# Gathering an expert's rows by quarters of channels and turning them on VectorE in squares of 32, in a fused attention and mixture-of-experts kernel

## The chip, the cores and the metric

The kernel runs on one core of a Trainium2 chip. The metric is the device time of one execution in microseconds (us), the median of several runs, each beside a run of the other kernel. The profiles shown are of one execution each; their times are measured from the first instruction to the last and are a little shorter than the device time.

The engines are named as in the profile: PE (TensorE, matrix products and transposes), PEld (its weight loads), DVE (VectorE), ACT (ScalarE), POOL (GpSimd) and SP (SyncE, which here only issues transfers). A fp32 product of one 128x128 block stands as two matmul instructions in the profile, so the counts there are twice those of the code; transposes stand once.

## The reference

Attention with a window of 96 tokens and 8 global tokens comes first (batch 4, 8 heads, 768 tokens, 64 channels per head), then a router that sends each of the 3072 tokens to one of 8 experts, then that expert's two matrix products. All data are fp32.

```python
def _attn_ref(q, k, v, n_global, n_local):
    ...
    scores = scale * np.matmul(q, k.transpose(0, 1, 3, 2))     # + bias by distance, masked
    a = np.exp(scores - max)                   # softmax over the kept keys
    return np.matmul(a / sum, v)

# x: attention's output as (3072 tokens, 512 channels)
def _moe_ref(x, expert_emb, tau, w1, w2):                      # w1: 8 x 512 x 1024, w2: 8 x 1024 x 512
    ...
    logits = xn @ en.T / tau                                   # rows of x and expert_emb normalized
    expert_idx = np.argmax(logits, axis=1)
    gate_w = probs[np.arange(N), expert_idx]                   # probs: softmax of logits
    for e in range(E):
        mask = expert_idx == e
        h = np.maximum(x[mask] @ w1[e], 0.0)
        out[mask] = gate_w[mask, None] * (h @ w2[e])
    return out
```

## The kernel before

Attention works through 32 steps (4 batches, 2 groups of heads, 4 parts). Beside them, each finished batch is turned to rows of tokens, divided by its softmax sums, stored to DRAM (`x_dram`), and routed. The router (`choose`) gives each token a slot in a table in DRAM (`meta`): expert times `SL` plus the token's rank in the expert. An entry has three numbers: row in x_dram, row in the output, gate. GpSimd scatters the entries.

```python
    slot = new([n], "slot", I32)
    nc.vector.scalar_tensor_tensor(out=slot, in0=best, scalar=16.0 * k.SL, in1=rank, op0=ALU.mult, op1=ALU.add)
    gate = new([n], "gate")
    nc.vector.reduce_sum(out=gate, in_=lg, axis=AX.X)
    nc.vector.tensor_scalar_add(gate, gate, 1e-9)
    mt = new([n, 3], "mt")
    nc.vector.reciprocal(out=mt[:, :, 2], in_=gate)
    nc.gpsimd.tensor_copy(out=mt[:, :, 0:2], in_=k.tok[:, b * k.NT + i0 : b * k.NT + i0 + n, :])
    for t in range(n):
        i = nc.gpsimd.indirect_dma_start(
            out=k.meta[:], out_offset=bass.IndirectOffsetOnAxis(ap=slot[:, t : t + 1], axis=0),
            in_=mt[:, t, :], in_offset=None,
        )
...
    def store_x(t, i, ps):
        xs = xs_p.tile([P, H, D], F32, name="xs", tag="xs")
        nc.vector.tensor_tensor(out=xs[:], in0=ps[:].rearrange("p (h d) -> p h d", d=D),
                                in1=t.rd[:, i, :].unsqueeze(2).broadcast_to([P, H, D]), op=ALU.mult)
        flat = xs[:].rearrange("p h d -> p (h d)")
        r0 = t.b * S + t.b // (B - 1) + i * P
        nc.sync.dma_start(k.x_dram[r0 : r0 + P, :], flat)
        nc.scalar.activation(k.junk[:], flat, AF.Square, accum_out=t.ss[:, i : i + 1])
```

The last batch is routed in two halves. Expert 0 takes its first 256 tokens (`FIRST`) as soon as the first three batches are routed; their first product fills TensorE while the last half is routed. `k.base` holds how many slots expert 0 has served that way.

```python
    def first_base():
        k.base = k.const.tile([P, E], F32, name="base")
        nc.vector.memset(k.base[:], 0.0)
        nc.vector.tensor_scalar(out=k.base[:, 0:1], in0=k.cnt[:, 0:1], scalar1=float(FIRST), scalar2=None, op0=ALU.min)
        k.si = k.const.tile([P, 1], I32, name="si")
        nc.vector.tensor_copy(out=k.si[:], in_=k.base[:, 0:1])

    def first_rows():
        k.first = Net()
        k.first.rows = load_rows(k, k.meta[0:FIRST, :], k.ea, k.ea2, FIRST // P, nc.gpsimd, k.ZR + 1)
        k.first.xT = k.ea.tile([P, k.NC, FIRST], F32, name="fxT")
        k.first.hT = k.ea.tile([P, k.NF, FIRST], F32, name="fhT")

    def first_turn():
        for j, xg in enumerate(k.first.rows[2]):
            ps = bank()
            for c in range(k.NC):
                nc.tensor.transpose(ps[:, c * P : (c + 1) * P], xg[:, c * P : (c + 1) * P], k.ident[:])
            nc.scalar.copy(out=k.first.xT[:, :, j * P : (j + 1) * P], in_=ps[:].rearrange("p (c n) -> p c n", c=k.NC))
...
    attend(*steps[-1])                       # the end of attention
    for hf in active:
        half_turns(hf)
    first_turn()
    hf = start_half(t, 1)                    # the last half batch
    xs = [turn_x(t, 3)]
    turn_sums(hf)
    score_experts(hf, bank())
    xs += [turn_x(t, 4), turn_x(t, 5)]
    for i in range(3):
        store_x(t, 3 + i, xs[i])
    ...
    turn_products(hf)
    first_product(0)
    next(hf.router)
    hf.router.send(bank())                   # L210 is in here
    first_product(1)
    next(hf.router)
    ...                                      # first_product(2) to (7)
```

Then the experts run one after the other. For each, the slots' entries are read, up to 512 rows (`CAP`) of x_dram are gathered by token in four tiles of 128 rows, and TensorE turns them to channels on the partitions (`xT`). A switch on the expert's count (`width`, a multiple of 32, or 128) takes a branch with just so many columns.

```python
def load_rows(k, slots, gp, xgp, NJ=CAP // P, cast=None, upto=None):

    nc = k.nc
    mt = gp.tile([P, NJ, 3], F32, name="emt", tag="emt")
    i = nc.sync.dma_start(mt[:], slots.rearrange("(j p) w -> p j w", p=P))
    for sc in k.scatters or []:
        ...                                  # waits for every scatter
    ids = gp.tile([P, NJ, 2], I32, name="ids", tag="ids")
    (cast or nc.vector).tensor_copy(out=ids[:], in_=mt[:, :, 0:2])
    xgs = []
    for j in range(NJ):
        xg = xgp.tile([P, k.DM], F32, name="xg", tag="xg")
        nc.gpsimd.indirect_dma_start(
            out=xg[:], out_offset=None, in_=k.x_dram[0 : upto or k.N + 1, :],
            in_offset=bass.IndirectOffsetOnAxis(ap=ids[:, j, 0:1], axis=0),
        )
        xgs.append(xg)
    return mt, ids, xgs


def turn_rows(k, rows, xT):

    for j, xg in enumerate(rows[2]):
        ps = k.work.tile([P, k.NC, P], F32, name="work", tag="work")
        for c in range(k.NC):
            k.nc.tensor.transpose(ps[:, c, :], xg[:, c * P : (c + 1) * P], k.ident[:])
        k.nc.vector.tensor_copy(out=xT[:, :, j * P : (j + 1) * P], in_=ps[:])
...
def expert(k, rows, xT, w1, w2, width=None, coming=None, behind=None):
    ...
    arms = [len(WIDTHS) - 1] if width is None else tc.Switch(width.index, len(WIDTHS), hint=width.hint)
    for arm in arms:
        w = WIDTHS[arm]
        parts = []
        for size in (64, 32):
            if w % (2 * size) >= size:
                parts.append(part_rows(k, rows, w // (2 * size) * 2 * size, size))
        for f2 in range(k.NF // 2):
            ps = k.big.tile([P, 2, CAP], F32, name="big", tag="big")
            for i in range(2):
                f = 2 * f2 + i
                for c in range(k.NC):
                    nc.tensor.matmul(ps[:, i, 0:w], lhsT=w1[:, c, f * P : (f + 1) * P], rhs=xT[:, c, 0:w],
                                     start=c == 0, stop=c == k.NC - 1)
            nc.scalar.activation(hT[:, 2 * f2 : 2 * f2 + 2, 0:w], ps[:, :, 0:w], AF.Relu)
        if coming:
            turn_rows(k, coming.rows, coming.xT)
        for part in parts:
            second_part(k, part, hT, w2)
        for j in range(0 if behind else 1, w // P):
            second(k, rows, hT, w2, j, k.work)
    if coming:
        coming.width = take_width(k, coming.e)
    if behind:
        behind()
    else:
        second(k, rows, hT, w2, 0, k.work0)
...
        def prepare(e):
            t = Net()
            t.e = e
            at = e * n.SL
            if e == 0:
                at = nc.values_load(n.si[0:1, 0:1], engines=(SP,), min_val=0, max_val=FIRST)
            t.rows = load_rows(n, n.meta[bass.ds(at, CAP), :], n.gp, n.xgp)
            ...                              # from expert 2 on: load its weights
            return t

        with tc.manual_schedule(engines=ORDERED | set(ARMS)):
            choose_widths(n)
            coming = prepare(0)
            coming.width = take_width(n, 0)
            second(n, n.first.rows, n.first.hT, n.w[0][1], 0, n.work)
            coming.xT = n.xtp.tile([P, n.NC, CAP], F32, name="xT", tag="xT")
            turn_rows(n, coming.rows, coming.xT)
            for e in range(n.E):
                now, coming = coming, prepare(e + 1) if e + 1 < n.E else None
                behind = None
                if e == 0:
                    def behind():
                        second(n, n.first.rows, n.first.hT, n.w[0][1], 1, n.work0)
                expert(n, now.rows, now.xT, *now.w, now.width, coming, behind)
```

`manual_schedule` keeps the program's order on each engine. `second` computes 128 rows of the second product on TensorE (L904), scales them by the gate on VectorE (L907) and scatters them to the output by GpSimd (L908); `second_part` does so for the last 64 or 32 rows (L939). If the inputs do not meet what the fast path assumes, a general path (`leftover`) recomputes; with the inputs here it is not entered.

## Time and profile before

| | |
|---|---|
| device time | 589.17 us (588.56 to 589.4, 3 runs) |
| profiled execution | 580.19 us, span 578.5 us |
| TensorE clock granted | 0.971 of full speed on average |
| attention and routing | 0 to 225 us |
| experts 0 to 7 | 225 to 562 us |
| DMA moved | 78.11 MB, 135 GB/s over the span |

Line 1 of the page gives each engine's busy time; line 2 cuts the span in 40 slices and gives the busy share in tenths. In a line of a group, "x128" is the number of instructions, then come busy time in us and mean ns of one, then the engine's idle time before them and what ended it ("<-"). In the chain of work that ended last, each line is a start, a length, and what the time was spent on; one line can merge many instructions.

### The profile page before, as it was taken

Reading aid. Unit: us, or ns where it says so; the run is one execution under the profiler, and the core shown is the slowest. Engines: PE = TensorE matmul, PEld = TensorE weight load, DVE = VectorE, ACT = ScalarE, POOL = GpSimd, SP = SyncE. Lnnn points to the kernel's source line nnn. Section 1 sums busy time; section 2 is a strip of 40 time slices with the busy share of each in tenths; the row PEclk is TensorE's granted clock in tenths of the full one; section 3 lists DMA queues with packets and bytes.
Section 4 is the critical chain, followed back from the end, with each engine's and each line's share of the span. In section 5 each row is a group of like instructions: output and inputs, shape, how many; then the busy total and the mean of one; then the engine's idle time right before and its main releaser. Section 6 shows DMA issues by size and latency. Waiting matters only on the chain.

```text
span 578.5 us, 9188 instructions
## 1 busy us (share of the span) xinstructions
PE 548.2 (95%) x3542; PEld 350.8 (61%) x3542; DVE 164.5 (28%) x411; ACT 142.3 (25%) x336; POOL 101.8 (18%) x130
## 2 busy tenths in 40 slices
PE   8899999999989798999999999999999999999980
PEld 8577788787767676757444447556556444645530
DVE  3254666675775412111000110212101110210010
ACT  4575756756643210001001001001001001001100
POOL 2000015013232225140130013030130130110010
PEclk9799999999989898999999999999999999999995
DMA  8999998994246414543460326443461460010000
GB/s 174 194 186 201 258 254 182 256 235 72 74 128 185 126 25 129 189 150 115 177 238 0 123 84 238 158 142 120 160 232 39 159 226 30 16 43 20 2 36 25
DMA packets 117331, 78.11 MB, mean 135 GB/s; under 512 B 92965, under 2 KB 101157, under 8 KB 117169
## 3 DMA queue, kind: packets, MB, share of 16 engines
q1 hardware_dynamic: 109744, 60.72, 40.9%
q0 software_dynamic: 5536, 15.25, 7.4%
q8 instruction: 51, 0.84, 0.6%
q14 instruction: 112, 0.91, 0.5%
q10 hardware_dynamic: 1888, 0.40, 0.4%
HBM read 63.38 MB, written 13.16 MB: 132 GB/s over the span
## 4 chain that ended last, share of the span: by engine, by line
PE 58%; issue 2%; DMA 1%; POOL 1%; DVE 0%; POOLq 0%
PE big L968 27%; PE work L904 25%; PE work L939 3%; PE work L894 2%; DMA xg<-x_dram,ids 1%; POOL xg L881 0%; POOL out_dram L908 0%; POOL meta L245 0%; DVE y L907 0%; POOLq L1004 0%; DVE flags L1018 0%; POOLq L908 0%; POOLq L881 0%
## 5 line engine op out<-in xcount | busy, mean ns | idle before, releaser
L968 PE MATMUL big<-xT,w1t 128*128 128x320 f32 (+5 forms) x512 | 159.0, 472 | 0.0
L904 PE MATMUL work<-w2t,hT 128*128 128x512 f32 x320 | 139.4, 595 | 0.0
L968 PEld LDWEIGHTS big<-xT,w1t 128*128 128x128 f32 x512 | 95.0, 193 | 64.4 <-issue 31.6
L904 PEld LDWEIGHTS work<-w2t,hT 128*128 128x128 f32 x320 | 60.3, 190 | 74.6 <-issue 73.8
L970 ACT ACTIVATE hT<-big 128x640 f32<-128x640 f32 (+5 forms) x32 | 24.9, 777 | 303.7 <-PE big L968 303.7
L429 DVE TENSOR_TENSOR ex<-ex,table 126x768 f32<-126x768 f32 x64 | 57.7, 904 | 57.9 <-ACT ex L422 55.9
L907 DVE TENSOR_SCALAR y<-work,emt 128x512 f32<-128x512 f32 x22 | 16.5, 751 | 156.7 <-PE work L904 150.0
L422 ACT ACTIVATE ex<-pa 126x384 f32<-126x384 f32 (+1 forms) x128 | 53.3, 476 | 28.8 <-PE pa L418 28.8
L908 POOL DMA_INDIRECT out_dram<-y,ids x22 | 21.8, 992 | 185.6 <-DVE y L907 133.1
L895 DVE COPY xT<-work 128x512 f32<-128x512 f32 x32 | 20.1, 683 | 109.9 <-PE work L894 109.9
L418 PE MATMUL pa<-qT,kT 64*126 64x192 f32 (+1 forms) x512 | 50.7, 336 | 0.4 <-ACT ex L422 0.4
L444 PE MATMUL od<-ex,v 126*64 126x192 f32 (+1 forms) x576 | 48.6, 316 | 0.0
L418 PEld LDWEIGHTS pa<-qT,kT 64*126 64x126 f32 x512 | 41.5, 190 | 10.7 <-issue 6.0
L444 PEld LDWEIGHTS od<-ex,v 126*64 126x64 f32 x576 | 36.0, 142 | 8.8 <-issue 4.7
L881 POOL DMA_INDIRECT xg<-x_dram,ids x34 | 33.3, 981 | 23.0 <-issue 15.6
L245 POOL DMA_INDIRECT meta<-mt,slot x24 | 26.3, 1095 | 38.3 <-DVE good L542 7.8
L452 PE MATMUL od<-ex,halves 126*32 126x192 f32 (+1 forms) x576 | 26.9, 310 | 0.0
L943 POOL DMA_INDIRECT out_dram<-y,pids x7 | 7.1, 1015 | 89.3 <-DVE y L942 84.0
L217 POOL TENSOR_TENSOR ss<-ss,half 128x3 f32<-128x3 f32 (+1 forms) x6 | 6.3, 1047 | 93.0 <-ACT junk L526 93.0
L526 ACT ACTIVATE junk<-xs 128x512 f32<-128x512 f32 x24 | 15.2, 632 | 27.1 <-DVE xs L521 22.2
L939 PE MATMUL work<-w2t,hT 128*32 128x128 f32 (+1 forms) x320 | 20.4, 317 | 0.0
L452 PEld LDWEIGHTS od<-ex,halves 126*32 126x32 f32 x576 | 14.9, 111 | 8.8 <-issue 3.6
(143 smaller groups left out, 389.9 us busy)
## 6 DMA issues: line engine op xcount, KB each, us to landing
w1t<-in_moe_w_dram SPq DMA_DIRECT2D x6, 2048.0 KB, 9.5
w2t<-in_moe_w_dram SPq DMA_DIRECT2D x6, 2048.0 KB, 11.5
v<-in_v_dram SPq DMA_DIRECT2D x32, 192.0 KB, 4.7
x_dram<-xs SPq DMA_DIRECT2D x24, 256.0 KB, 2.8
k<-in_k_dram SPq DMA_DIRECT2D x28, 192.0 KB, 4.0
q<-in_q_dram SPq DMA_DIRECT2D x28, 192.0 KB, 4.2
w1t<-in_moe_w_dram SPq DMA_DIRECT2D x32, 128.0 KB, 3.7
w2t<-in_moe_w_dram SPq DMA_DIRECT2D x32, 128.0 KB, 3.7
```

Source lines behind the costliest of these rows:

```text
L245: i = nc.gpsimd.indirect_dma_start(out=k.meta[:], out_offset=bass.IndirectOffsetOnAxis(ap=slot[:, t : t + 1], axis=0), in_=mt[:, t, :], in ...
L418: nc.tensor.matmul(u.sp[e][0:ROWS, a * n : (a + 1) * n], lhsT=t.kT[rows, j, 0:ROWS], rhs=t.qT[rows, j * BLK : j * BLK + n], start=True, st ...
L422: nc.scalar.activation(u.ex[:, e], u.sp[e][0:ROWS, 0 : 2 * u.n].rearrange("p (a c) -> p a c", a=2), AF.Exp, scale=k.scale)
L429: nc.vector.tensor_tensor(out=exv, in0=exv, in1=tab[:, :, 0 : u.n // BLK, :], op=ALU.mult)
L444: nc.tensor.matmul(g.od[a][e * D : (e + 1) * D, at : at + c1 - c0], lhsT=g.v[0:ROWS, 2 * a + e, u.j, :], rhs=u.ex[:, e, a, c0:c1], start=f ...
L452: nc.tensor.matmul(g.od[2][32 * i : 32 * i + 32, at : at + c1 - c0], lhsT=k.halves[0:ROWS, g.m].rearrange("p i c -> p (i c)"), rhs=u.ex[:, ...
L881: nc.gpsimd.indirect_dma_start(out=xg[:], out_offset=None, in_=k.x_dram[0 : upto or k.N + 1, :], in_offset=bass.IndirectOffsetOnAxis(ap=id ...
L904: nc.tensor.matmul(ps[:], lhsT=hT[:, f, j * P : (j + 1) * P], rhs=w2[:, f, :], start=f == 0, stop=f == k.NF - 1)
L908: nc.gpsimd.indirect_dma_start(out=k.out[:, :], out_offset=bass.IndirectOffsetOnAxis(ap=ids[:, j, 1:2], axis=0), in_=y[:], in_offset=None, ...
L939: nc.tensor.matmul(ps[i * size : (i + 1) * size, 0:m], lhsT=hT[:, f, base : base + size], rhs=w2[:, f, i * m : (i + 1) * m], start=f == 0, ...
L968: nc.tensor.matmul(ps[:, i, 0:w], lhsT=w1[:, c, f * P : (f + 1) * P], rhs=xT[:, c, 0:w], start=c == 0, stop=c == k.NC - 1)
L970: nc.scalar.activation(hT[:, 2 * f2 : 2 * f2 + 2, 0:w], ps[:, :, 0:w], AF.Relu)
```

## The change

An expert's rows are no longer turned by TensorE but by VectorE, which transposes squares of 32 x 32 within groups of 32 partitions. For that to give xT, each group of 32 partitions must hold its own quarter of the channels for 32 tokens. So (1) the rows are gathered in sixteen transfers, each of which brings 32 tokens in four quarter rows of 128 channels (512 bytes), on 4 x 32 partitions; (2) x_dram holds the channels in an order in which a quarter row carries the right 32 of each block of 128, which `store_x` writes in two instructions; (3) the slots of each 256 are stored in an order in which eight entries for one partition lie side by side (`place`), so that the table is read in runs of 96 bytes, four times over, and the entries in slot order (`mt`) are copied from it by four small VectorE instructions; (4) expert 0's own rows and the 256 first ones are still gathered whole and turned by TensorE, after a copy on ScalarE that puts their channels in order (`in_order`); (5) expert 0's second read of the table starts at a static slot (256), for which its count is raised to at least 256 and the table has 256 more slots per expert; (6) the turning of the next expert's rows is issued just ahead of the last tile of `tiles` instead of straight after the first product.

The aim is to take the transposes of experts 1 to 7 off TensorE. The diff, with the general path and pool set-up cut:

```diff
@@ -22,6 +22,7 @@
 PIECES = 32
+UNIT = 256
 FIRST = 256
@@ -75,6 +76,11 @@
     nc.gpsimd.tensor_scalar_add(k.tok[:, last:, 0], k.tok[:, last:, 0], 1.0)
+    k.quad = pool.tile([P, 1], F32, name="quad")
+    nc.gpsimd.memset(k.quad[:], 0.0)
+    for q in range(1, 4):
+        nc.gpsimd.memset(k.quad[32 * q : 32 * q + 32], float(q))
     k.cnt = pool.tile([P, k.E], F32, name="cnt")
@@ -234,6 +240,7 @@
     nc.vector.scalar_tensor_tensor(out=slot, in0=best, scalar=16.0 * k.SL, in1=rank, op0=ALU.mult, op1=ALU.add)
+    slot = place(k, slot, new)
@@ -255,6 +262,17 @@
+def place(k, slot, new):
+    nc = k.nc
+    low, mid = new([slot.shape[1]], "low", I32), new([slot.shape[1]], "mid", I32)
+    nc.vector.tensor_scalar(out=low, in0=slot, scalar1=31, scalar2=3, op0=ALU.bitwise_and, op1=ALU.logical_shift_left)
+    nc.vector.tensor_scalar(out=mid, in0=slot, scalar1=5, scalar2=UNIT // 32 - 1, op0=ALU.logical_shift_right, op1=ALU.bitwise_and)
+    nc.vector.scalar_tensor_tensor(out=mid, in0=slot, scalar=-UNIT, in1=mid, op0=ALU.bitwise_and, op1=ALU.bitwise_or)
+    nc.vector.tensor_tensor(out=low, in0=low, in1=mid, op=ALU.bitwise_or)
+    return low
...
@@ -517,10 +537,12 @@
     def store_x(t, i, ps):
-        xs = xs_p.tile([P, H, D], F32, name="xs", tag="xs")
-        nc.vector.tensor_tensor(out=xs[:], in0=ps[:].rearrange("p (h d) -> p h d", d=D),
-                                in1=t.rd[:, i, :].unsqueeze(2).broadcast_to([P, H, D]), op=ALU.mult)
-        flat = xs[:].rearrange("p h d -> p (h d)")
+        xs = xs_p.tile([P, k.DM], F32, name="xs", tag="xs")
+        flat = xs[:]
+        for e in range(2):
+            dst = flat.rearrange("p (e l c j) -> p e c l j", e=2, l=2, c=4)[:, e]
+            nc.vector.tensor_tensor(out=dst, in0=ps[:].rearrange("p (c e l j) -> p e c l j", c=4, e=2, l=2)[:, e],
+                                    in1=t.rd[:, i, e::2].unsqueeze(2).unsqueeze(3).broadcast_to([P, 4, 2, 32]), op=ALU.mult)
         r0 = t.b * S + t.b // (B - 1) + i * P
@@ -562,11 +584,11 @@
     def first_base():
         k.base = k.const.tile([P, E], F32, name="base")
         nc.vector.memset(k.base[:], 0.0)
-        nc.vector.tensor_scalar(out=k.base[:, 0:1], in0=k.cnt[:, 0:1], scalar1=float(FIRST), scalar2=None, op0=ALU.min)
-        k.si = k.const.tile([P, 1], I32, name="si")
-        nc.vector.tensor_copy(out=k.si[:], in_=k.base[:, 0:1])
+        nc.vector.memset(k.base[:, 0:1], float(FIRST))
+        nc.vector.tensor_tensor(out=k.cnt[:], in0=k.cnt[:], in1=k.base[:], op=ALU.max)
@@ -577,8 +599,10 @@
             ps = bank()
+            xo = k.ea.tile([P, k.DM], F32, name="xo", tag="xo")
+            in_order(k, nc.scalar, xo[:], xg[:])
             for c in range(k.NC):
-                nc.tensor.transpose(ps[:, c * P : (c + 1) * P], xg[:, c * P : (c + 1) * P], k.ident[:])
+                nc.tensor.transpose(ps[:, c * P : (c + 1) * P], xo[:, c * P : (c + 1) * P], k.ident[:])
             nc.scalar.copy(out=k.first.xT[:, :, j * P : (j + 1) * P], in_=ps[:].rearrange("p (c n) -> p c n", c=k.NC))
...
@@ -864,34 +891,71 @@
-def load_rows(k, slots, gp, xgp, NJ=CAP // P, cast=None, upto=None):
-    nc = k.nc
+def load_rows(k, slots, gp, xgp, NJ=CAP // P, cast=None, upto=None, squares=False):
+    nc, U = k.nc, UNIT // 32
+    cast = cast or nc.vector
+    mq = gp.tile([P, NJ * P // UNIT, U, 3], F32, name="mq", tag="mq")
+    for u in range(NJ * P // UNIT):
+        src = slots[u * UNIT : (u + 1) * UNIT, :].rearrange("(i g) w -> i (g w)", g=U)
+        i = nc.sync.dma_start(mq[:, u].rearrange("p g w -> p (g w)"), src.unsqueeze(0).to_broadcast([4, 32, U * 3]))
+        for sc in k.scatters or []:
...
     mt = gp.tile([P, NJ, 3], F32, name="emt", tag="emt")
-    i = nc.sync.dma_start(mt[:], slots.rearrange("(j p) w -> p j w", p=P))
-    for sc in k.scatters or []:
...
+    mqv = mq[:].rearrange("p u (h a) w -> p (u h) a w", a=4)
+    for a in range(4):
+        rows = slice(32 * a, 32 * a + 32)
+        cast.tensor_copy(out=mt[rows], in_=mqv[rows, :, a, :])
     ids = gp.tile([P, NJ, 2], I32, name="ids", tag="ids")
-    (cast or nc.vector).tensor_copy(out=ids[:], in_=mt[:, :, 0:2])
+    cast.tensor_copy(out=ids[:], in_=mt[:, :, 0:2])
+    src = k.x_dram[0 : upto or k.N + 1, :]
+    if squares:
+        qid = gp.tile([P, NJ * 4], I32, name="qid", tag="qid")
+        cast.tensor_scalar(out=qid[:], in0=mq[:].rearrange("p u g w -> p (u g) w")[:, :, 0], scalar1=4.0,
+                           scalar2=k.quad[:], op0=ALU.mult, op1=ALU.add)
+        xq = xgp.tile([P, NJ * 4, P], F32, name="xq", tag="xq")
+        for g in range(NJ * 4):
+            nc.gpsimd.indirect_dma_start(
+                out=xq[:, g], out_offset=None, in_=src.rearrange("t (q m) -> (t q) m", q=4),
+                in_offset=bass.IndirectOffsetOnAxis(ap=qid[:, g : g + 1], axis=0),
+            )
+        return mt, ids, xq
     xgs = []
...
         nc.gpsimd.indirect_dma_start(
-            out=xg[:], out_offset=None, in_=k.x_dram[0 : upto or k.N + 1, :],
+            out=xg[:], out_offset=None, in_=src,
             in_offset=bass.IndirectOffsetOnAxis(ap=ids[:, j, 0:1], axis=0),
...
+def in_order(k, eng, dst, xg):
+    src = xg.rearrange("p (q c j) -> p c q j", q=4, j=32)
+    dst = dst.rearrange("p (c q j) -> p c q j", q=4, j=32)
+    (eng.copy if eng is k.nc.scalar else eng.tensor_copy)(out=dst, in_=src)
 def turn_rows(k, rows, xT):
+    if not isinstance(rows[2], list):
+        n = CAP // 32 // 4
+        for i in range(4):
+            g = slice(i * n, (i + 1) * n)
+            dst = xT[:].rearrange("p c (g i) -> p g c i", i=32)[:, g]
+            k.nc.vector.transpose(dst, rows[2][:, g].rearrange("p g (c j) -> p g c j", j=32))
+        return
     for j, xg in enumerate(rows[2]):
+        xo = k.yp.tile([P, k.DM], F32, name="xo", tag="xo")
+        in_order(k, k.nc.scalar, xo[:], xg[:])
         ps = k.work.tile([P, k.NC, P], F32, name="work", tag="work")
         for c in range(k.NC):
-            k.nc.tensor.transpose(ps[:, c, :], xg[:, c * P : (c + 1) * P], k.ident[:])
+            k.nc.tensor.transpose(ps[:, c, :], xo[:, c * P : (c + 1) * P], k.ident[:])
         k.nc.vector.tensor_copy(out=xT[:, :, j * P : (j + 1) * P], in_=ps[:])
@@ -968,11 +1032,16 @@
             nc.scalar.activation(hT[:, 2 * f2 : 2 * f2 + 2, 0:w], ps[:, :, 0:w], AF.Relu)
-        if coming:
+        tiles = range(0 if behind else 1, w // P)
+        for i, part in enumerate(parts):
+            if coming and not tiles and i == 0:
+                turn_rows(k, coming.rows, coming.xT)
+            second_part(k, part, hT, w2)
+        if coming and not tiles and not parts:
             turn_rows(k, coming.rows, coming.xT)
-        for part in parts:
-            second_part(k, part, hT, w2)
-        for j in range(0 if behind else 1, w // P):
+        for j in tiles:
+            if coming and j == tiles[-1]:
+                turn_rows(k, coming.rows, coming.xT)
             second(k, rows, hT, w2, j, k.work)
...
@@ -1069,7 +1138,8 @@
-    k.gp, k.xgp, k.xtp = pool("gp", 3), pool("xgp", 6), pool("xtp", 2)
+    k.gp, k.xgp, k.xtp = pool("gp", 3), pool("xgp", 2), pool("xtp", 2)
+    k.xgq = pool("xgq", 4)
     k.hp, k.yp, k.rp = pool("hp", 2), pool("yp", 4), pool("rp", 4)
@@ -1104,7 +1174,7 @@
     n.x_dram = tc.dram_tile([n.N + 1, n.DM], F32, name="x_dram")
-    n.SL = n.N + CAP
+    n.SL = n.N + CAP + FIRST
     n.ZR = n.N - n.S
@@ -1132,10 +1202,8 @@
             t.e = e
-            at = e * n.SL
-            if e == 0:
-                at = nc.values_load(n.si[0:1, 0:1], engines=(SP,), min_val=0, max_val=FIRST)
-            t.rows = load_rows(n, n.meta[bass.ds(at, CAP), :], n.gp, n.xgp)
+            at = e * n.SL + (FIRST if e == 0 else 0)
+            t.rows = load_rows(n, n.meta[at : at + CAP, :], n.gp, n.xgp if e else n.xgq, squares=e > 0)
             if e < 2:
```

## The prediction, written before the changed kernel was seen to run

> **What bounds the kernel now.** I read the page first, then the chain of work that ended last in order of time, then the timeline around the passage from attention to experts.
>
> ```profile
> PE 548.2 (95%) x3542; PEld 350.8 (61%) x3542; DVE 164.5 (28%) x411; ACT 142.3 (25%) x336; POOL 101.8 (18%) x130
> ...
> DVE  3254666675775412111000110212101110210010
> ...
> PE 58%; issue 2%; DMA 1%; POOL 1%; DVE 0%; POOLq 0%
> ...
> L895 DVE COPY xT<-work 128x512 f32<-128x512 f32 x32 | 20.1, 683 | 109.9 <-PE work L894 109.9
> ...
> L881 POOL DMA_INDIRECT xg<-x_dram,ids x34 | 33.3, 981 | 23.0 <-issue 15.6
> ```
>
> TensorE is the bound, and in the second half of the span, where the experts run, VectorE and GpSimd are nearly idle. The chain gives the stages of that half; it starts at the last scatter of slots and holds nothing but TensorE from 224.5 us on:
>
> ```profile
> 219.80 4.53 DMA xg<-x_dram,ids
> ...
> 225.55 9.90 PE big L968 x64
> 235.45 1.88 PE work L894 x16
> 237.33 1.89 PE work L939 x64
> 239.22 13.93 PE work L904 x32
> 253.16 17.23 PE big L968 x64
> 270.38 1.88 PE work L894 x16
> ```
>
> Each expert is a first product (L968), the turning of the next expert's rows (L894, 16 transposes, 1.88 us), then the second product (L939, L904). The turning stands seven times in this chain behind a first product (1.88 us five times, 1.94 and 1.95 us), with no gap on either side.
>
> The passage before it (187 to 225 us) is another matter: TensorE has gaps there, and the end is set by a chain through every engine. The timeline, (start, duration):
>
> ```profile
> 187.45 1.09 PE L581 MATMUL pa<-ident,xg 128*128 128x128 f32 x8
> 188.98 0.22 ACT L229 ACTIVATE lg<-lg 128x24 f32<-128x24 f32 x1 [1.56 <-DVE lg L228]
> 189.11 1.05 ACT L582 COPY fxT<-pa 128x512 f32<-128x512 f32 x2
> 190.97 0.63 ACT L526 ACTIVATE junk<-xs 128x512 f32<-128x512 f32 x1 [0.34 <-DVE xs L521]
> 194.22 0.69 DVE L521 TENSOR_TENSOR xs<-pa,rd 128x512 f32<-128x512 f32 x1 [2.75 <-DMA x_dram<-xs]
> 196.84 0.59 PE L210 MATMUL pa<-oh,prefix 128*128 128x24 f32 x2 [3.67 <-DVE oh L204]
> ```
>
> TensorE turns the first 256 rows at 187.45 without waiting, although ScalarE is still held by L229 until 189.2; then come the transposes for the last rows of x, and 3.67 us of waiting for the router (L210). What is put in front of that wait delays the last scatter, the table read and the gathers for expert 0.
>
> [...] all 34 gathers stand on POOL at 981 ns each. So quarter rows cost four times the gathers, on an engine with room. [...]
>
> **The change part by part.**
>
> 1. Turning of experts 1 to 7 leaves TensorE: 5 x 1.88 + 1.94 + 1.95 = **-13.3 us**, all on the chain. The second product that now follows directly must find hT ready: the ScalarE eviction after the last first-product matmul takes 0.44 to 1.02 us (L970), and the first part needs the last quarter of hT only after 1.4 us (three quarters of 1.89) or more. No new wait there. [...] for experts 1 to 6 two tiles of 6.9 us remain after the point at which they are issued, so they are hidden if the rows are there.
>
> 2. First turn (attention's end). ScalarE must now first reorder each of the two row tiles, SBUF to SBUF, 512 elements: I take 0.63 us, the duration of L526 of the same size. In program order they stand behind L229, so the first begins at 189.2, not 187.45. With a single xo buffer, and ScalarE's order copy, evict, copy, evict: copy to 189.86, four transposes to 190.5, eviction (about 0.55) to 191.15, copy to 191.78, transposes to about 192.4. TensorE goes on to the last rows of x at 192.35 instead of 188.3: **4 us later**, and the router chain behind it moves along, except that VectorE's own backlog (until 189.9) gives a little back and the split store costs 0.15 us more. I put **+3.9 us**.
>
> 3. Expert 0's table. Its address becomes static: the read that took 1.32 us to issue becomes two of about 0.37 us, of 256 pieces instead of 512; I take -0.5 us. Against it four small copies and a cast on VectorE stand where one cast of 0.16 us stood: 0.6 us more. **+0.1 us**.
>
> 4. Expert 0's rows are still turned by TensorE, after a ScalarE copy. The last gather landed at 219.80 + 4.53 = 224.33; copy and hand-over put **+0.75 us** on it.
>
> 5. Gathers for expert 1. They run one after the other at 1.27 us (227.12, 228.39, 229.64, 230.89), so 16 take 19 us to the start of the last. The cast in front was at 226.20, one instruction; it becomes six, 0.8 us more. Counted from the start of expert 0's first product T0 (225.5): first gather at T0 + 2.4, last at T0 + 21.4, landing 5.7 (median here) to 7.2 us (median of all) later, transposed by T0 + 27.7 to 29.2. Expert 0 without its turning ends at T0 + 9.90 + 1.89 + 13.93 = T0 + 25.7. So expert 1 would wait 2 to 3.5 us if its first product needs all four transposes, nothing if it needs only the 320 columns it reads (twelve gathers, 5 us earlier). In expert 0 the first product starts at 225.47, before the last eviction of xT at 225.59, so columns do count there; across the branches of a switch I can't tell. I choose **+2 us**. Later experts last 34.8 us or more (17.23 + 3.6 + 13.93), so theirs are ready by about 28, hidden. The same holds for expert 2, although its gathers begin some 7 us into expert 1 because VectorE is held by expert 1's.
>
> 6. Attention. store_x becomes two instructions of 256 elements: the evictions of 384 and 512 elements take 0.55 and 0.69 us, so 256 take about 0.42, and the pair 0.15 us more than one; x24 = 3.7 us of VectorE. The slot order adds four tiny operations to each of six router steps, 0.2 us apart: 4.8 us. In the last step they are hidden, since the slot is ready at 200.3 and ScalarE's exponential only at 203.04. The rest lies beside a TensorE that is busy 40.00 of 40 us in 60 to 100 us; I let a sixth of it through: **+1.5 us**.
>
> Sum: -13.3 + 3.9 + 0.1 + 0.75 + 2 + 1.5 = -5.05. 589.17 - 5.05 gives **584 us**.
>
> **Rivals.**
>
> A. *The clean gain.* The passage absorbs the ScalarE copies (L210 already waits 3.67 us) and expert 1 finds its rows: -13.3 + about 2 = 578, at best 576. For it: TensorE's certain saving. Against it: that wait is for the router chain, which itself lies behind the delayed transposes; slack of TensorE is not slack of the chain.
>
> B. *GpSimd becomes the bound of short experts.* Gathers per expert rise from 5 to 20.3 us plus scatters of 1.3 us each; small transfers may land later beside the 4 MB of weights per expert (over 400 GB/s in stretches). If each landing took 10 us more, expert 1 would wait 12 us and the others still little: 590 to 596. Against it: the 64 KB that a gather brings stay the same per 1.27 us, about 50 GB/s.
>
> C. *VectorE transposes of 4-byte data are slow.* At 2.5 us each, four take 10 us; two tiles (13.9 us) hide them in most experts, but expert 1 would wait another 2 and expert 7 nothing: about 587. At 5 us each every expert would wait some 6 us and the kernel would be past 610. Nothing in this trace speaks to it[...].
>
> **Range and chances.** Without terms 5 and 6 and with half of term 2 the sum is -10.4 (579); with 5 at 3.5, 6 at 4 and term 2 as it is, -1 (588). Widened for B and C: 577 to 591. Faster by over 2% means under 577.4 and needs nearly all of A: 0.14. Slower by over 2% (over 601) needs C at its worst or B in every expert: 0.04. Within 2%: 0.82.
>
> **What would show it.** The turning group on TensorE (L894) should fall from 128 to 16 instructions; the 8 of the first turn (L581) stay. POOL's busy time should rise by 84 x 0.95 = 80 us to about 182. [...] The wait of the last router step (L210) should begin some 4 us later and the first product of expert 0 start near 230 us. Expert 1's first product should show a gap of 0 to 3.5 us, with VectorE's transpose or a gather as releaser, and no other expert a gap. Step 1 would be wrong if TensorE waits behind any first product; step 2 if its stream resumes before 191 us; step 6 if attention reaches its last attend step (186 us) more than 3 us late.

## The result, and the profile after

The kernel after takes **620.15 us** (median of 4 runs, 619.58 to 621.88); the kernel before, beside it, 588.87 us. The ratio is **1.0545**, 95% interval 1.0508 to 1.0583: slower by 5.5%, where 584 us with a range of 577 to 591 was predicted.

These lines of the page after answer to those of before: the busy times, the shares of the chain that ended last, and two groups.

```profile
PE 553.1 (89%) x3430; PEld 343.0 (55%) x3430; DVE 175.2 (28%) x498; ACT 146.2 (24%) x342; POOL 181.2 (29%) x222
...
PE 72%; issue 7%; another core or an unknown queue 6%; SPq 4%; DVE 3%; DMA 3%; ACT 2%; POOL 0%; ACTq 0%; POOLq 0%; DVEq 0%
...
L921 POOL DMA_INDIRECT xq<-x_dram,qid x112 | 106.1, 947 | 37.8 <-issue 37.5
...
L1003 PE MATMUL work<-w2t,hT 128*32 128x128 f32 (+1 forms) x320 | 32.6, 364 | 30.1 <-issue 19.4
```

GpSimd is as busy as was worked out (181.2 us, predicted 182). TensorE runs 112 instructions fewer, yet its share of the span falls from 95 to 89%. Two things are new: 6% of the chain has no releaser in this trace ("another core or an unknown queue"; there is one core), and a group of TensorE's own matmuls (L1003, the narrow parts of the second product) has 19.4 us of "issue" ahead of it, time in which nothing that the profile shows was waited for.

Expert 3 shows both. First the chain of work in order of time (start, duration):

```profile
372.47 13.64 PE big L1032 x48
386.12 0.02 issue
386.14 0.70 ACT hT L1034
386.84 13.52 another core or an unknown queue
400.37 0.02 issue
400.39 0.71 ACT hT L1034
```

The last line is ScalarE's eviction of the fourth quarter of hT. The matmuls that it waits for are all in this group of TensorE's timeline, which ends at 389.70; the eviction starts 10.69 us later:

```profile
372.31 17.39 PE L1032 MATMUL big<-xT,w1t 128*128 128x320 f32 x64
389.63 2.59 PE L1003 MATMUL work<-w2t,hT 128*64 128x256 f32 x21
392.52 0.38 PE L1003 MATMUL work<-w2t,hT 128*64 128x256 f32 x1 [0.30 <-issue]
394.63 0.38 PE L1003 MATMUL work<-w2t,hT 128*64 128x256 f32 x1 [1.73 <-issue]
396.05 0.58 PE L1003 MATMUL work<-w2t,hT 128*64 128x256 f32 x1 [1.05 <-issue]
401.15 1.98 PE L1003 MATMUL work<-w2t,hT 128*64 128x256 f32 x8 [4.51 <-ACT hT L1034]
```

The reader is to see that TensorE itself slows down after 392 us: single matmuls whose operands have been ready since 386.84, with up to 1.7 us between them, and then the 8 that need the late quarter. All the while GpSimd issues its 16 gathers for the next expert, one every 1.25 us, the first at 377.42 and the last at 396.20. The last record of the train's landing is at 398.46, and at 400.39 the late eviction starts.

The same can be worked out for every expert: the start of each of the four hT evictions less the end of the matmuls that it waits for, in us, and beside it the length of the expert (start of its first product to that of the next):

```
expert        0      1      2      3      4      5      6
before: all 28 evictions start 0.04 to 0.10 us after their matmuls
after, lags of the four evictions
  1st       0.04   0.04   0.10   0.10   0.10   0.10   0.10
  2nd       0.04   0.04   0.04   0.04   0.04   0.04   0.04
  3rd       1.08   2.41   4.34   0.75   0.04   0.04   6.59
  4th       6.09   8.09   0.04  10.69   9.29   7.10   1.01
length, us
  before    27.5   36.7   57.1   36.7   40.2   43.4   53.9
  after     42.3   42.3   54.9   46.2   47.5   46.0   52.0
```

(The run with 12 arithmetic operations below, which is the kernel before on a chip that has the delay, also has no lag over 0.10 us.) Expert 7, which has no gathers beside it, has no lag and takes 41.5 us in both. Experts 2 and 6, the longest, become shorter: there the train ends while the first product still runs (last gather issued at 340.65 and 534.79, last matmul of the product done at 345.01 and 537.96). The short ones become longer by 2.6 to 14.8 us. TensorE's clock adds to it: after the single matmuls the granted clock is 0.50 from 396.1 to 406.3 us, 1.00 on both sides of it, and a 128x512 matmul takes 1.06 us in that stretch and 0.59 after it. In the 3.6 us before the drop (392.5 to 396.1) TensorE is busy for 0.80 us. Why the clock drops there was not tested.

### The profile page after: what moved, and what is told of

The parts are those of the page before. It is cut to its first block, busy times and chain, and to the rows that moved or that the text cites. A ratio compares the mean times of both kernels' runs of the same rounds, so it can differ in the third digit from the quotient of the medians.

```text
span 620.2 us, 9177 instructions
## 1 busy us (share of the span) xinstructions
PE 553.1 (89%) x3430; PEld 343.0 (55%) x3430; DVE 175.2 (28%) x498; ACT 146.2 (24%) x342; POOL 181.2 (29%) x222
## 4 chain that ended last, share of the span: by engine, by line
PE 72%; issue 7%; another core or an unknown queue 6%; SPq 4%; DVE 3%; DMA 3%; ACT 2%; POOL 0%; ACTq 0%; POOLq 0%; DVEq 0%
PE work L968 23%; PE big L1032 20%; PE od L464 6%; PE pa L438 5%; PE work L1003 4%; PE od L472 3%; PE pa L419 3%; PE pa L613 2%; SPq L387 2%; DMA q<-in_q_dram 2%; PE pa L536 1%; ACT hT L1034 1%; SPq L394 1%; PE pa L219 1%
## 5 line engine op out<-in xcount | busy, mean ns | idle before, releaser
L968 PE MATMUL work<-w2t,hT 128*128 128x512 f32 x320 | 144.8, 612 | 2.8 <-ACT hT L1034 2.8
L921 POOL DMA_INDIRECT xq<-x_dram,qid x112 | 106.1, 947 | 37.8 <-issue 37.5
L968 PEld LDWEIGHTS work<-w2t,hT 128*128 128x128 f32 x320 | 62.4, 197 | 82.5 <-issue 78.3
L1034 ACT ACTIVATE hT<-big 128x640 f32<-128x640 f32 (+5 forms) x32 | 24.7, 777 | 329.3 <-PE big L1032 228.1
L1003 PE MATMUL work<-w2t,hT 128*32 128x128 f32 (+1 forms) x320 | 32.6, 364 | 30.1 <-issue 19.4
L1003 PEld LDWEIGHTS work<-w2t,hT 128*32 128x32 f32 (+1 forms) x320 | 17.2, 136 | 45.0 <-issue 27.8
L252 POOL DMA_INDIRECT meta<-mt,low x24 | 25.9, 1079 | 40.2 <-DVE lg L528 7.0
L1006 DVE TENSOR_SCALAR y<-work,pgate 128x256 f32<-128x256 f32 (+1 forms) x7 | 3.0, 426 | 109.1 <-PE work L1003 109.1
```

The lines of the kernel that those rows point to most:

```text
L252: i = nc.gpsimd.indirect_dma_start(out=k.meta[:], out_offset=bass.IndirectOffsetOnAxis(ap=slot[:, t : t + 1], axis=0), in_=mt[:, t, :], in ...
L921: nc.gpsimd.indirect_dma_start(out=xq[:, g], out_offset=None, in_=src.rearrange("t (q m) -> (t q) m", q=4), in_offset=bass.IndirectOffsetO ...
L968: nc.tensor.matmul(ps[:], lhsT=hT[:, f, j * P : (j + 1) * P], rhs=w2[:, f, :], start=f == 0, stop=f == k.NF - 1)
L1003: nc.tensor.matmul(ps[i * size : (i + 1) * size, 0:m], lhsT=hT[:, f, base : base + size], rhs=w2[:, f, i * m : (i + 1) * m], start=f == 0, ...
```

## The experiments

The edits are shortened; what stands in brackets or after "then" describes code that is left out.

The theory after reading the two traces, **T**: a long train of gathers on GpSimd holds up TensorE's completions, and with them ScalarE's evictions and TensorE's own stream. Its first rival, **W**: it is a matter of what the changed kernel waits for (rows that land late, transposes behind VectorE's order, the new place of the turning).

### Extra gathers in the kernel before

If T holds, the kernel before must show the delay when it gets the gathers and nothing else of the change. For each expert from 1 on, 12 more gathers go into a tile that nobody reads, a quarter row per partition in the first run and a whole row in the second:

```diff
+    if extra:                                   # 12 for experts 1 to 7
+        spare = k.spare_p.tile([P, extra, P], F32, name="spare", tag="spare")   # second run: [P, extra, k.DM]
+        for g in range(extra):
+            nc.gpsimd.indirect_dma_start(out=spare[:, g], in_=(x_dram as quarter rows),   # second run: whole rows
+                in_offset=bass.IndirectOffsetOnAxis(ap=ids[:, g % 4, 0:1], axis=0))
```

> The kernel before, with twelve more gathers of quarter rows (512 bytes) per expert 1 to 7 into a spare tile that nobody reads; TensorE still turns the rows, and nothing waits for the extra gathers. Theory T (a long train of gathers on GpSimd holds up TensorE and what waits for TensorE): gaps in TensorE of 4 to 15 us in most experts, about 620 us. Rival W (the stalls come from the changed order of waits, the rows of the next expert arriving late or VectorE's transposes): no gaps, 589 us give or take 3.

> As the run with twelve quarter-row gathers, but the extra twelve bring whole rows (2 KB). If the number of gathers in a row matters and not the size of a piece: the same gaps, about 620 us or a little more for the traffic. If the small pieces of 512 bytes are to blame: near 589 us. If nothing but waits matters (rival W): 589 us.

Measured, beside 584.93 us of the kernel before on this chip: 634.20 us, ratio 1.0825 (1.0676 to 1.0973), and 632.95 us, ratio 1.0803 (1.066 to 1.0947). The lags are of the kind of the kernel after (fourth eviction of expert 0: 14.37 and 14.94 us late, of expert 1: 8.05 and 8.16 us late, of expert 3: 8.02 and 8.01), and experts 0, 1, 3, 4 and 5 take 42.9 to 49.3 us. So W falls: with no square, no other order and no VectorE transpose in the kernel, the delay is there. Nor is it the bytes here: four times as many give the same ratio within 0.003.

### Fewer gathers in the kernel after

Both runs **leave work out**: of each expert's 512 rows only the first quarter (4 gathers) or the first half (8 gathers) is fetched, and the transposes take these again for the rest. All other instructions stay.

```diff
-        for g in range(NJ * 4):
+        for g in range(4):                      # second run: 8
@@ turn_rows
-            k.nc.vector.transpose(dst, rows[2][:, g]...)
+            k.nc.vector.transpose(dst, rows[2][:, slice(i * n % 4, i * n % 4 + n)]...)   # second run: % 8
```

> The kernel after with only the first four of the sixteen gathers per expert 1 to 7 (three quarters of each expert's rows are left out; all four transposes read the same 128 rows' worth of tile). Theory T: no train, no gaps, so the gain of 13 us from TensorE shows against a passage that is some 5 us later: 580 to 585 us. Rival W: the order of waits is the same, so the gaps stay, above 610 us; if only late arrival was the cause, 580 to 585 as well.

> The kernel after with the first eight of the sixteen gathers per expert (half of the rows left out). Theory T with a backlog that builds up only after some five to ten gathers: 582 to 592 us, gaps in few experts. If the loss is in proportion to the number of gathers: about 600 us.

Measured on the same chip: 573.11 us, ratio 0.9782 (0.9642 to 0.9922), and 569.85 us, ratio 0.9726 (0.9593 to 0.986), both faster than was expected. With 4 gathers the only lag is 1.10 us, in expert 0. With 8 there are lags of 1.1 to 2.2 us in experts 1, 3 and 4 that cost nothing (these experts last as long as with 4 gathers) and of 4.59 us in expert 0, which takes 29.8 us instead of 24.6. The experts' lengths are what the change was meant to bring: 34.8, 54.9, 34.8, 38.4, 41.2 and 52.0 us for 1 to 6.

### Is it GpSimd's being busy, or the gathers?

Three variants of the extra work in the kernel before: 12 arithmetic operations on GpSimd instead of the gathers; 12 gathers of 16 rows instead of 128; 12 gathers of 128 rows with an operation of 1.36 us after each. And the kernel after with its 16 gathers cut into 8 and 8, with five such operations (7 us) between.

```diff
+    k.fil = pool.tile([P, 6], F32, name="fil")                   # fill, in all but the second
+        for _ in range(extra):                                   # first
+            nc.gpsimd.tensor_tensor(out=k.fil[:], in0=k.fil[:], in1=k.fil[:], op=ALU.pow)
+                out=spare[0:16, g], ... ap=ids[0:16, g % 4, 0:1]  # second
+            (gather of 128 quarter rows, then the pow)            # third
@@ kernel after, load_rows                                        # fourth
         for g in range(NJ * 4):
+            for _ in range(5 if g == NJ * 2 else 0):
+                (the pow)
```

> The kernel before, with twelve small arithmetic operations on GpSimd (a power of 128x6 elements, about 1.4 us each) behind the four gathers of each expert 1 to 7, in place of the twelve extra gathers: GpSimd is as busy, but moves nothing. If a busy GpSimd alone holds up TensorE: gaps, 620 us or more. If it takes the gathers: no late hT, 585 to 590 us.

> The kernel before with twelve extra gathers per expert of 16 rows each instead of 128 (512 bytes each). If the number of pieces (descriptors) makes the backlog: no gaps, 585 to 592 us. If the number of gather instructions or of their completions does: still about 630 us.

> The kernel before with twelve extra gathers of 128 quarter rows per expert, a power of 128x6 elements after each, so that they start every 2.7 us instead of every 1.27. If a backlog builds up because gathers follow too close: no late hT, 585 to 592 us. If every gather costs TensorE a fixed piece of time or gathers queue whatever their pace: 615 us or more.

> The kernel after, all sixteen gathers, but in two trains of eight with five powers of 128x6 on GpSimd (some 7 us) between them; nothing is left out. If a train of eight is harmless as in the run with eight gathers alone: TensorE streams on from expert 1 on, expert 1 starts late by some 8 us since its last rows come later, and the whole is 578 to 590 us. If the total of gathers per expert counts: 610 us or more.

Measured, beside 586.53 us of the kernel before on this chip:

- 12 operations: 586.41 us, ratio 0.9995 (0.9978 to 1.0012), no lag. GpSimd's being busy (212.4 us in all) costs nothing here.
- 12 gathers of 16 rows: 634.71 us, ratio 1.0826 (1.0733 to 1.0919), the lags of the full gathers. With 12 gathers of 128 quarter rows it was 1.0825, so an eighth of the rows brings the same delay; the number of gather instructions is what the two share.
- 12 paced gathers: no late eviction beyond 0.96 us in expert 0, but 628.38 us, ratio 1.0718 (1.0635 to 1.0801). The delay is gone and another cost has come: GpSimd's queue runs late, and with it the next rows. In expert 3 the first gather of the rows that are needed starts 19.2 us after the expert (384.68 after 365.47), with arithmetic alone 2.5 us after it. TensorE's timeline in expert 3 of this run:

```profile
388.16 1.08 PE L904 MATMUL work<-ident,xg 128*128 128x128 f32 x4 [5.31 <-DMA xg<-x_dram,ids]
389.56 1.11 PE L904 MATMUL work<-ident,xg 128*128 128x128 f32 x4 [0.32 <-DMA xg<-x_dram,ids]
```

  TensorE waits for the gathered rows themselves: the 5.31 us have a releaser in the trace, which the late eviction of expert 3 in the kernel after has not.
- 8 and 8 with 7 us between: no late eviction from expert 1 on; 610.94 us, ratio 1.0421 (1.0315 to 1.0526), outside of the 578 to 590 that was expected. The second train ends too late (expert 1 starts at 260.2 and lasts about 35 us when nothing holds it, but its gathers run from 274.9 to 284.6 and from 291.8 to 301.6), so the next experts wait for rows: 46.4 us for expert 1, 63.4 for expert 6.

So with pauses no eviction was late from expert 1 on in either run, and the time was lost elsewhere: 1.0718 and 1.0421 of before.

### An earlier table, to make room for a pause

In the kernel after the reads and casts of the table stand between the start of an expert and GpSimd's train, which begins 2 to 5.5 us into it. Here the table of expert e+2 is read and cast while expert e+1's rows are fetched. The gathers go out as 8, a pause of two operations (2.7 us), 8; or four by four with a pause of 1.36 us; or in one train.

```diff
+def read_table(...):     # the reads and casts of load_rows
+def fetch_rows(...):     # its gathers
+            for _ in range({8: 2}.get(g, 0)):        # second: {4: 1, 8: 1, 12: 1}, third: {}
+                nc.gpsimd.tensor_tensor(out=k.fil[:], in0=k.fil[:], in1=k.fil[:], op=ALU.pow)
-    k.gp, ... = pool("gp", 3), ...
+    k.gp, ... = pool("gp", 4), ...
+            look_up(1)                                # after expert 0's gathers
             for e in range(n.E):
                 now, coming = coming, prepare(e + 1) ...
+                look_up(e + 2)
```

> The kernel after with nothing left out; each expert's table is read and cast one expert earlier, so that the gathers can start as soon as an expert starts, and the 16 gathers go out as 8, a pause of two arithmetic operations on GpSimd (2.7 us), and 8. Theory (a long train of gathers holds up TensorE's completions): no hT eviction more than 2 us late, the last gather out about 25 us after the expert's start, so no late rows but in expert 1: 570 to 580 us, below both kernels. Rival (the pause needs to be as long as the 7 us tried, or the delay goes by the number of gathers of an expert, whatever the pause): evictions late by 5 to 10 us again and 600 us or more.

> As the run with 8 and 8, but with a pause of one arithmetic operation (1.36 us) after every four gathers. Theory: what counts is how many gathers stand in a row without a pause, so no late evictions and 570 to 580 us. Rival (the pause must give the chip time to empty what has piled up): three pauses of 1.36 us empty less than 16 gathers pile up, evictions 3 to 8 us late in the last third of the train, about 590 to 610 us.

> The early table alone, with all 16 gathers in one train. Theory: the same delays as in the kernel after, one or two evictions late by 5 to 10 us in most experts, 605 to 625 us; only the pause cures it. Rival (the delays come from where the train lies in the expert, late because the table is late): an earlier train meets no eviction that matters, under 585 us.

Measured, beside 579.26 us of the kernel before on this chip: 578.09 us, ratio 0.9969 (0.9947 to 0.9992); 581.39 us, 1.0037 (1.0006 to 1.0069); and the one that should have been slow, one train of 16: **567.45 us, 0.9801** (0.9765 to 0.9837), with not one lag over 0.10 us. Against the theory's words ("only the pause cures it") this is a miss. Two readings were left: the early table takes the delay away, or this chip does not have it.

### The same kernels on another chip

So the unchanged kernel after, the early table with one train, and a version that reads early but casts right before the gathers, as the kernel after does, ran together:

```diff
@@ third run: fetch_rows
-    mt, ids, qid = table
+    mt, ids, qid = cast_table(k, table)      # emt, ids and qid are made here, not in read_table
```

> The kernel after unchanged, on the chip on which the early table runs again, so that a difference of the chips is not taken for one of the kernels. If the delays come from the train and the late table, 5 to 6% over the kernel before, evictions late by 5 to 10 us. If they belong to some chips only, no late evictions, near 575 us.

> The run with the early table and one train of 16 gathers, again. If the early table takes the delays away: no late evictions, ratio about 0.98. If it was the chip: evictions late by 5 to 10 us here, if the unchanged kernel beside it has them too, and 605 us or more.

> The table is read one expert early, but cast on VectorE right before the gathers, as in the kernel after. If the read in front of the train matters: no late evictions, ratio about 0.98. If the casts in front of the train (VectorE's signal on which GpSimd then waits) matter: late evictions by 5 to 10 us and over 600 us.

Measured, beside 587.29 us of before: 616.09 us, ratio 1.048 (1.0423 to 1.0537); **621.79 us, 1.0578** (1.0544 to 1.0613); 614.35 us, 1.045 (1.0404 to 1.0496). All three have the lags. The early table does nothing for the delay; the chips differ. The same program, the same expert 3, the last three evictions in ScalarE's timeline, first on the chip of the section before:

```profile
351.82 0.70 ACT L1052 ACTIVATE hT<-big 128x640 f32<-128x640 f32 x1 [3.54 <-PE big L1050]
356.13 0.70 ACT L1052 ACTIVATE hT<-big 128x640 f32<-128x640 f32 x1 [3.60 <-PE big L1050]
360.43 0.70 ACT L1052 ACTIVATE hT<-big 128x640 f32<-128x640 f32 x1 [3.60 <-PE big L1050]
```

and on this one:

```profile
379.17 0.70 ACT L1052 ACTIVATE hT<-big 128x640 f32<-128x640 f32 x1 [3.54 <-issue]
384.11 0.70 ACT L1052 ACTIVATE hT<-big 128x640 f32<-128x640 f32 x1 [4.24 <-PE big L1050]
398.27 0.70 ACT L1052 ACTIVATE hT<-big 128x640 f32<-128x640 f32 x1 [13.46 <-remote]
```

In both the gathers follow one another every 1.25 us and start 5 us into the expert (348.30 after 343.0; 375.42 after 370.4).

The two traces differ in one thing more, the records of landings that they hold. Below are the gathers of the two traces; the figure at the end is the median time from issue to landing, and the second trace, where records are missing, has none:

```profile
xq<-x_dram,qid POOLq DMA_INDIRECT x112, 2.5
xq<-x_dram,qid POOLq DMA_INDIRECT x112
```

On the first chip 111 of the 112 gathers have 16 records of their landing, on this one none has, and the mean is 3.2 (all transfers of the program together: 6658 records and 4688). The traces of the kernel after (3.1 for a gather of its trains) and of every experiment outside the first chip lack records, most of all within long trains: the 12 extra whole-row gathers have 3.0 on average, the 12 paced ones 15.4. So the traces that show the delay are also short of records, most of all in their trains. That leaves a rival which no run here tests: the recording itself may bring the delay. Every timed run lists the granted clock of its execution, so each was recorded, and none tells what an unrecorded execution takes.

Hence the runs with pauses of the section before tell only what a pause costs where there is nothing to cure: 10.6 us (578.09 - 567.45) and 13.9 us.

### Pauses and fewer gathers on a chip that has the delay

Three runs side by side: the kernel after with the first 256 rows of an expert by quarters (8 gathers) and the others as two whole rows, turned by TensorE as in the kernel before; the early table with 8, 2.7 us, 8, again; and the unchanged kernel after as the control.

```diff
@@ first run: load_rows
-        for g in range(NJ * 4):
+        for g in range(NJ * 2):
             (quarter gather)
+        for j in range(NJ // 2, NJ):
+            (whole gather by ids[:, j, 0:1] into xgw)
@@ turn_rows
-        for i in range(4): (VectorE transpose)
+        for i in range(2): (VectorE transpose)
+        then tiles 2 and 3 by ScalarE's copy, TensorE's transposes and VectorE's eviction
```

> The kernel after, with nothing of the computation left out, but each expert's first 256 rows alone come by quarters (8 gathers, two VectorE transposes); the other 256 come as two whole-row gathers and are turned by TensorE, as before. 10 gathers in the train instead of 16. Theory (the delay grows with the number of gathers in a row): at most one eviction an expert late, by under 2 us, half of the saving on TensorE (about 7 us) kept, ratio 0.98 to 0.995 of before. Rival (any train beyond the 4 gathers of before is held against TensorE in proportion): a third to a half of the delays of after, ratio 1.01 to 1.03.

> The early table with 8 gathers, a pause of 2.7 us, and 8 gathers again, now beside the unchanged kernel after on the same chip. Theory: a pause empties what has piled up, so evictions late by under 2 us where the kernel after has 5 to 10, ratio 0.98 to 1.00. Rival (only the number of gathers in an expert counts, or 2.7 us is too short): delays as in the kernel after, ratio 1.04 or more.

> The kernel after unchanged, as the control on this chip. If this chip shows the delays: ratio about 1.05 and evictions late by 5 to 10 us. If not: ratio about 0.98.

Measured, beside 587.37 us of before: **581.03 us, 0.9885** (0.9862 to 0.9908); 592.19 us, 1.0093 (1.0059 to 1.0127); control 617.90 us, 1.0515 (1.0449 to 1.0582).

The control has the delay (fourth eviction of expert 3: 9.18 us late). The run with the pause has none over 1.33 us from expert 1 on (expert 0 has lags of 1.26, 3.49 and 1.65 us), and experts 1, 2, 3, 5 and 6 have exactly the lengths of the run that left 3/4 of the rows out: 34.8, 54.9, 34.8, 41.2, 52.0. So a pause of 2.7 us takes away most of the delay, beginning with expert 1. The run does not reach 0.98 because experts 0 and 4 take 37.9 and 47.6 us instead of 24.6 and 38.4, 22.5 us together. In expert 4 a scatter of results holds GpSimd's queue, so the gathers start late; two lines of GpSimd's timeline and two of TensorE's in this run:

```profile
399.78 0.98 POOL L990 DMA_INDIRECT out_dram<-y,ids  x1 [8.34 <-issue]
401.07 0.98 POOL L939 DMA_INDIRECT xq<-x_dram,qid  x1 [0.31 <-issue]
```

```profile
422.43 1.13 PE L1021 MATMUL work<-w2t,hT 128*32 128x128 f32 x4 [0.89 <-issue]
424.61 0.39 PE L1021 MATMUL work<-w2t,hT 128*32 128x128 f32 x1 [1.06 <-issue]
```

The second train (413.8 to 423.6) lies on the second product, where TensorE again runs in single matmuls; the pause has thinned the delay, not abolished it. Why that scatter waits 8.34 us stays open.

The half-and-half run beats both kernels, though with lags of 1.8 to 3.9 us on the third eviction of experts 1, 3, 4 and 5 (harmless) and of 7.41 us in expert 0, which takes 33.8 us. The last run adds a pause to it; it ran on another chip, with the kernel before alone beside it:

```diff
         for g in range(NJ * 2):
+            for _ in range({5: 2}.get(g, 0)):
+                nc.gpsimd.tensor_tensor(out=k.fil[:], in0=k.fil[:], in1=k.fil[:], op=ALU.pow)
```

> Half of the rows by quarters (8 gathers) and half whole (2 gathers), as before, with a pause of two arithmetic operations on GpSimd (2.7 us) after the fifth gather; nothing of the computation left out. Theory: trains of five with a pause between them are held against nothing, no eviction over 1 us late from expert 1 on; the delays that are left in the run without the pause go, and no expert waits for its rows: 0.97 to 0.98 of before. Rival (what is left there comes of something else, such as the whole-row gathers or TensorE's turning): no change, 0.985 to 0.99.

Measured: 583.42 us beside 586.78, ratio 0.9958 (0.994 to 0.9976). The theory's signs came (no lag over 0.10 us from expert 1 on, 0.72 in expert 0), its time did not: it is slower than even the rival said. And the signs prove less than they seem to: nothing with the delay ran on this chip. Its trace lacks records as those of the chips with the delay do (9.3 on average for a quarter gather), so it may have it too, which is not shown. Experts 1 to 6 last 35.6, 56.0, 35.6, 39.4, 42.4 and 53.2 us, as without the pause: in experts 1 to 6 nothing is gained. Expert 0 takes 36.6 us instead of 33.8, since the pause moves its train and TensorE stands waiting for the rows (4.92 us before the first transpose). Here the pause cost 2.8 us in expert 0, and the lags that it took away elsewhere had cost nothing.

Nor is the half-and-half run's gain what was expected. Its experts 0 to 7 take 337.4 us together, the kernel before 337.0. The gain lies after the last matmul: there GpSimd's closing drain takes 2.20 us instead of 7.18. By the number of gathers and scatters in the program it takes: 87 of them 7.18 us (before, and two runs on two other chips), 115 0.81, 129 2.20 (half and half, on two chips), 171 5.87 (after, and twelve runs on five chips), but 4.24 in the run whose 84 extra gathers have 16 rows. The difference of 5.0 us is most of the gain of 6.3.

## Why the prediction was wrong, step by step

The profiled execution of before (580.19 us; the timed runs beside the kernel after took 586.32 to 589.4) had a short attention: its end is at 186.65 us, in the five runs of variants with the same attention at 193 to 195 us. Its trace has all 16 records of each of its 34 gathers, as on the chip without the delay, where before takes 579.26 us. So the passage below is compared with the run with 12 arithmetic operations, whose passage is that of before. All in us.

**Part 1, turning off TensorE: predicted -13.3, and "No new wait there". The size is right, the second half is the step that failed.** Undisturbed, experts 0 to 6 take 280.7 (24.6, 34.8, 54.9, 34.8, 38.4, 41.2, 52.0, from the run with 4 gathers; experts 1 to 6 the same with all 16 on the chip without the delay) instead of 295.5: **-14.8**. About 1.0 of this is no turning: in the profile of before the clock is at 0.50 until 227.6, and expert 0's first product takes 9.90 us instead of 8.93. The kernel after takes 331.2: **+50.5** of delays on top, 17.7 in expert 0, 11.4 in 3, 9.1 in 4, 7.5 in 1, 4.8 in 5. The argument looked at the time of ScalarE's eviction and took for granted that it starts when its matmuls end, as in the kernel before. It starts up to 10.69 us later, and TensorE, which should have gone straight on, waits for it or creeps on in single matmuls. -14.8 + 50.5 = +35.7 of the experts' time.

**Part 2, the first turn, +3.9: right.** The first turn's last transpose starts 5.7 after attention's end instead of 1.6, and L210 3.6 later. TensorE's and ScalarE's lines after:

```profile
196.44 0.65 PE L605 MATMUL pa<-ident,xo 128*128 128x128 f32 x4 [2.24 <-ACT xo L941]
198.29 1.12 PE L605 MATMUL pa<-ident,xo 128*128 128x128 f32 x4 [1.20 <-ACT xo L941]
...
206.95 0.40 PE L216 MATMUL pa<-oh,prefix 128*128 128x24 f32 x2 [1.86 <-DVE oh L210]
```

The step waits for ScalarE's copy (0.60 and 0.62 us, taken as 0.63). 0.9 of the 3.6 is taken up again before the last scatter.

**Part 3, expert 0's table, +0.1: wrong in size.** From the last scatter to the first cast it takes 5.71 instead of 7.96: **-2.25**. SyncE issues the read 2.33 us after the last scatter, in the compared run 5.46, so this alone gives about 3.1 us where 0.5 was put. That the static address did it is likely and was not tested on its own. The four small copies take 0.70 us of it back.

**Part 4, the copy on the last rows, +0.75: right**, 0.87 (last gather to first product 6.33 instead of 5.46). Parts 2 to 4 together: 3.6 - 0.9 - 2.25 + 0.87, about **+1.4** (measured whole, from attention's end to expert 0: 39.41 instead of 38.04) against 4.75.

**Part 5, gathers for expert 1, +2 and "hidden" for later experts: wrong.** It counted trains only as a time until rows are ready. For that the counting was good: the last gather of expert 1 starts at T0 + 20.8 (predicted 21.4), and on the chip without the delay they land 2.5 us after issue, sooner than thought; with 8, 2.7 us, 8 there, the last gather ends at T0 + 20.7 and expert 1 starts at T0 + 24.7. The predicted T0 + 27.7 to 29.2 holds 0.6 us for VectorE's transposes, an estimate of the author's that nothing in the trace before showed. What happens on ScalarE and TensorE while a train runs was in no term.

**Part 6, attention, +1.5: nothing there.** It ends at 193.33 instead of 193.15.

**Not foreseen:** the closing drain, 5.87 instead of 7.18.

Sum: -14.8 + 50.5 + 1.4 + 0.2 - 1.3 = +36.0; the profiled spans differ by 35.0 (620.2 against 585.2 of the compared run), the medians by 31.3. (In the prediction's range, the sum without terms 5 and 6 and with half of term 2 is -10.5, not -10.4.)

**The rivals.** B was nearest in its name, GpSimd as the limit of short experts, and not in its mechanism: it let the rows land 10 us late. In expert 3 after, the last gather is issued at 396.20 and the last record of its landing is at 398.46; what is late is the eviction, at 400.39, after matmuls that ended at 389.70. C falls: the VectorE transpose, which the trace before did not show, takes 0.67 us, where C put 2.5 or 5.

```profile
L951 DVE STREAM_TRANSPOSE xT<-xq x28: 667/669/702, 259.9 to 553.0; 128x512 f32<-128x512 f32 x28
```

A would have been near the truth on the chip without the delay, where the early-table version runs at 0.98 of before.

**Of the signs that the prediction named**, the counts came (16 transposes of experts' rows left on TensorE, GpSimd 181.2), the first turn went on after 191, and expert 0 started at 232.74 instead of near 230, mostly because attention ended later than in the profiled execution of before. The sign against step 1, TensorE waiting behind a first product, is there in five experts of eight.

**What stays open.** Shown: the number of gathers in a row brings the delay (16 after: up to 10.69 us; 4: 1.10), neither their bytes (1.0825 and 1.0803) nor their rows (1.0826), nor GpSimd's being busy (0.9995); a pause of 2.7 us takes most of it away (1.33 us at most from expert 1 on); it is there in the result and on four of the chips that ran the experiments, on one it is not, and on the last run's nothing tells. Not shown: by which way the train holds up the evictions and TensorE's stream, what is different on the chip without it beyond its nearly complete records of landings, and whether the delay is there in an execution that is not recorded. The kernel after itself did not run on that chip.

## What to carry to other kernels

When a change multiplies the DMA instructions of one engine, count the longest train of them in a row, and look what the other engines do while it runs: GpSimd, with room by its busy time (29% of the span after), brought 50.5 us of delays here with trains of 16 where 4 had been. In a trace the sign is an eviction that starts microseconds after the matmuls it waits for, with no releaser or "issue" ahead of it, and single matmuls with gaps beside it; measure it with a train of useless gathers in the old kernel before building the new one. Run the candidate on more than one chip with the old kernel beside it: one chip alone would have shown 0.98 here for a version that loses 6% on another. Look whether a page gives its DMAs a time to landing: the page after has none in the eight groups that it lists (3.1 records of landing for a gather of its trains), the page of before has one in all eight (16 for each of its gathers).

## What the runs showed of the hardware

- On the chips with the delay, and in recorded executions, which are all there are here: trains of 16 gathers on GpSimd, one every 1.25 us, go with evictions up to 14.9 us late against their matmuls (4 with 12 extra whole-row gathers, fourth eviction of expert 0); 4 with at most 1.1 us; 8 with up to 4.6; 10 with up to 7.4.
- It is the same for gathers of 16 rows and of 128, of 512 bytes and of 2048 a row (1.0826, 1.0825 and 1.0803 of before); 12 arithmetic operations on GpSimd in place of the extra gathers do nothing (0.9995).
- The same program differed by 54 us between two chips (567.45 and 621.79) whose times for the kernel before differ by 8 (579.26 and 587.29). The slower one's trace holds 4688 records of landings, the other's 6658.
- GpSimd's drain at the program's end takes 0.81 to 7.18 us by the number of indirect transfers issued (115: 0.81, 129: 2.20, 171: 5.87, 87: 7.18), not in step with it; 171 of which 84 have 16 rows: 4.24.
